# One fixed step list for all engines of a fused attention and gMLP kernel, with its own buffer rings, contiguous-write transposes, masks by affine select on GpSimd, and v by a casting DMA

## The chip, the cores and the metric

The kernel runs on one core of one Trainium2 chip. The time is device time of that core, in microseconds (us). Most executions of one kernel lie within a few per cent (the kernel before 244.14 to 247.13 us). An execution more than 1.5% above the fastest of its kernel is called slow here, and the ratios use fast runs alone.

The engines are named as in the profile: PE (the tensor engine's matmuls), PEld (its weight loads), DVE (VectorE), ACT (ScalarE), POOL (GpSimd), SP (SyncE, which only issues DMAs here). Each engine has its own list of instructions here, and the engines wait for each other by semaphores: in the kernel before, GpSimd waited 62.7 us in all at one line (L301) for results of DVE. A wait also holds up what stands behind it in the list. So the order in which a program is written down for one engine can cost time on another.

## The reference, cut

Sliding-window attention with four sink keys feeds a gated MLP whose gate mixes along the sequence. Shapes: 4 batches, 8 heads, 768 positions, head size 64, so a model width of 512.

```python
# attention, per batch and head: q, k, v are (768, 64)
scores = q @ k.T / sqrt(64)
keep   = (key < 4) | ((0 <= query - key) & (query - key < 128))
a      = softmax(where(keep, scores, -1e9))
x      = heads_side_by_side(a @ v)              # (4, 768, 512)

# gMLP
h      = gelu_tanh(x @ w_in)                    # 512 -> 1024
u, v   = h[..., :512], h[..., 512:]
v_n    = (v - mean(v)) / sqrt(var(v) + 1e-6) * g_ln
v_s    = einsum('ts,bsd->btd', w_sg, v_n) + b_sg[None, :, None]   # w_sg is 768 x 768
out    = x + (u * v_s) @ w_out
```

## The kernel before

The kernel computes in bf16 with float32 sums. A helper for each stage is called in interleaved Python loops; the framework then reorders instructions by its own scheduler and gives out buffers from pools. Heads go in pairs `p`, 0 to 3. `T` makes the transposed q and k of a pair, `QK` the scores and their exponentials, `AV` the attention output, `MV` and `MU` the two halves of the first MLP layer, `WT` the transposed `w_sg`, `SP` the product with it, `OUT` the last layer.

```python
ps_sc = ctx.enter_context(tc.tile_pool(name="ps_sc", bufs=2, space=bass.MemoryType.PSUM))  # 2 banks each
ps_av = ctx.enter_context(tc.tile_pool(name="ps_av", bufs=2, space=bass.MemoryType.PSUM))
ps_mm = ctx.enter_context(tc.tile_pool(name="ps_mm", bufs=2, space=bass.MemoryType.PSUM))

def T(b, p):
    q32, k32, v32 = staged.pop((b, p))          # float32, loaded by SyncE's queue
    for name, src in (("q", q32), ("k", k32)):
        cb = cast.tile([128, NT, 2, Dh], BF16, name=name + "b")
        pcast(cb..., src...)                    # GpSimd: float32 -> bf16          [cut]
        ps = ps_mm.tile([128, NT, 128], BF16, name="trp", tag="mm")
        for t in range(NT):                     # NT = 6
            nc.tensor.transpose(ps[:, t, :], cb[:, t, :, :].rearrange("p h d -> p (h d)"), iden)
        dst = trs.tile([128, S], BF16, name=name + "T")
        dv = dst.rearrange("p (i t) -> p t i", t=NT)     # row 6*i + t sits at i*6 + t
        if name == "q":
            nc.vector.tensor_copy(dv, ps)
        else:
            nc.scalar.copy(dv, ps)
    pcast(v_sb[b % 2][:, 2 * p:2 * p + 2, :, 0:Dh], v32...)   # GpSimd casts v       [cut]
    # ... sink columns of k: 2 small DVE copies

def QK(b, p, g):
    # ... matmuls into sc, two PSUM banks
    nc.scalar.activation(out=pt[:, :, 0:w], in_=sc[:, :, 0:w], func=AF.Exp, scale=scale)
    m = (mask0 if g == 0 else mask1)[:, 0:w]
    nc.vector.tensor_mul(pt[:, :, 0:w], pt[:, :, 0:w], m.unsqueeze(1).to_broadcast([128, 2, w]))

def MV(b, jj):
    # ... matmuls into hp
    nc.scalar.activation(out=vt, in_=hp, func=AF.Gelu_apprx_tanh)
    # ... bn_stats and bn_aggr on DVE -> mv; (var + 1e-6) ** -0.5 on GpSimd -> rs
    for jl in range(2):
        nc.vector.tensor_scalar(out=z[b][:, 2 * jj + jl, :], in0=vt[:, jl, :],
                                scalar1=mv[:, jl, 0:1], scalar2=rs[:, jl:jl + 1],
                                op0=ALU.subtract, op1=ALU.mult)

# the order, for each batch b [cut]
for n, m in enumerate(mu):          # mu: 3 x MV(b), 4 x MU(b)
    m()
    if n >= 2 and tu:
        tu.pop(0)()                 # tu: T of the next batch
if b == 0:
    for ti in range(NT):
        WT(ti)
# ... then the list of QK, AV, XT of batch b+1, mixed evenly with the SP and OUT of batch b
```

A row of q is loaded so that each partition holds six neighbouring positions, and the transposes put position 6*i + t into column i of block t. The copy to SBUF must restore the natural order. It reads the PSUM tile in order and writes each 2-byte value 12 bytes after the one before it.

The softmax here doesn't subtract the row's maximum and nothing guards it: scores larger than these inputs give would overflow.

## Time and profile before

The median was 245.59 us of 3 runs (244.14 to 247.13).

| | before |
|---|---|
| median of 4 | 246.18 us |
| span of the profiled run | 245.3 us |
| mean granted TensorE clock | 0.900 of full |
| busy PE / DVE / ACT / POOL | 74 / 73 / 55 / 39% |
| first matmul | 6.65 us |
| first matmul of the first MLP layer | 42.7 us |

The page of the kernel before opens with the busy time of each engine. Then comes the chain that ended last: the shares of the span by engine, and below that by line, when one goes back from the last instruction and asks at each step what released it.

```profile
PE 182.6 (74%) x1460; PEld 99.1 (40%) x1460; DVE 178.5 (73%) x302; ACT 135.2 (55%) x123; POOL 96.5 (39%) x134
...
DVE 37%; PE 27%; ACT 13%; POOL 8%; issue 6%; DMA 5%; SPq 2%; POOLq 0%; DVEq 0%; ACTq 0%
DVE qT L168 10%; DVE pt L206 9%; ACT kT L170 7%; PE hv L254 6%; PE ops L307 6%; POOL gatedT L301 5%; DVE z L271 5%; DMA v_104<-in_v_dram 4%; DVE gtmp L298 4%; ACT pt L204 4%; PE sc L199 3%; DVE st L265 3%; PE vs L294 3%; DVE ot L310 3%; PE scs L184 2%
```

No engine is close to full, and the chain changes engines all the time. That is the picture of engines that wait for one another in turn, DVE in front.

The groups of that page: line, engine, operation, output and input, shapes, number; after the first bar, busy us and mean ns of one; after the second, the idle time of that engine just before and what ended it.

```profile
L168 DVE COPY qT<-trp 128x768 bf16<-128x768 bf16 x16 | 43.5, 2718 | 12.4 <-PE trp L164 12.2
L170 ACT COPY kT<-trp 128x768 bf16<-128x768 bf16 x16 | 43.6, 2725 | 13.8 <-PE trp L164 13.8
...
L244 ACT COPY xT<-xps 128x768 bf16<-128x768 bf16 x16 | 12.8, 803 | 26.6 <-PE xps L243 26.6
...
L206 DVE TENSOR_TENSOR pt<-pt,mask_128 128x1024 bf16<-128x1024 bf16 (+1 forms) x32 | 25.8, 817 | 0.9 <-ACT pt L204 0.4
```

The same kernel's groups by form hold a further copy of the same size, on DVE, with contiguous bf16 on both sides in the inner dimension:

```profile
L335 DVE COPY wsgT<-wps 128x768 bf16<-128x768 bf16 x6 | 3.3, 558 | 2.4 <-PE wps L333 2.3
```

The q and k copies (L168, L170) take 2.72 us each. Two other copies of exactly 128x768 bf16 from PSUM take 0.80 us on ACT (L244) and 0.56 us on DVE (L335). What sets the q and k copies apart is the step of their writes.

A table of stretches, cut at the first MLP matmul of each batch. Columns: the stretch, its length, busy us of PE, PEld, DVE, ACT, POOL (instructions), granted clock, DMA share, GB/s.

```profile
0.00:42.70 42.70, 22.22 (x203) 12.72 (x204) 28.08 (x43) 26.03 (x23) 22.69 (x44) 0.88 1.00 236
42.70:105.80 63.10, 50.59 (x420) 29.42 (x419) 49.53 (x84) 34.42 (x32) 27.75 (x33) 0.84 0.59 157
105.80:160.50 54.70, 44.03 (x358) 23.20 (x356) 42.80 (x73) 33.36 (x30) 21.47 (x26) 0.88 0.32 92
160.50:211.60 51.10, 40.40 (x359) 22.23 (x356) 41.61 (x73) 33.09 (x30) 14.64 (x18) 0.97 0.09 32
211.60:245.30 33.70, 25.36 (x128) 11.56 (x125) 16.52 (x33) 8.29 (x9) 9.90 (x14) 0.98 0.16 58
```

In the two steady stretches (105.8 to 211.6) PE and DVE are each busy 84.4 us of 105.8. Each waits a fifth of the time, though not at the same moments.

### The profile page before, as it was taken

Reading aid. Unit: us, or ns where it says so; the run is one execution under the profiler, and the core shown is the slowest. Engines: PE = TensorE matmul, PEld = TensorE weight load, DVE = VectorE, ACT = ScalarE, POOL = GpSimd, SP = SyncE. Lnnn points to the kernel's source line nnn. Section 1 sums busy time; section 2 is a strip of 40 time slices with the busy share of each in tenths; the row PEclk is TensorE's granted clock in tenths of the full one; section 3 lists DMA queues with packets and bytes.
Section 4 is the critical chain, followed back from the end, with each engine's and each line's share of the span. In section 5 each row is a group of like instructions: output and inputs, shape, how many; then the busy total and the mean of one; then the engine's idle time right before and its main releaser. Section 6 shows DMA issues by size and latency. Waiting matters only on the chain.

```text
span 245.3 us, 3835 instructions
## 1 busy us (share of the span) xinstructions
PE 182.6 (74%) x1460; PEld 99.1 (40%) x1460; DVE 178.5 (73%) x302; ACT 135.2 (55%) x123; POOL 96.5 (39%) x134
## 2 busy tenths in 40 slices
PE   0457557892959979798478869898559698978892
PEld 0234333551634445445232336544234365534340
DVE  2775976788785789739993989739996888466553
ACT  2493768495953545166957736166979263455000
POOL 8619406526620645405750612413303315012550
PEclk9999875798575999999855999999889999999999
DMA  7969999999900028198700012120000030300033
GB/s 198 264 123 322 209 225 311 304 296 312 268 5 0 0 85 236 46 274 199 194 0 3 0 47 85 43 88 0 0 0 3 0 128 3 128 1 3 1 128 128
DMA packets 39778, 28.59 MB, mean 117 GB/s; under 512 B 26576, under 2 KB 36048, under 8 KB 39760
## 3 DMA queue, kind: packets, MB, share of 16 engines
q1 hardware_dynamic: 37920, 25.60, 37.2%
q0 software_dynamic: 1840, 2.75, 6.2%
q8 instruction: 11, 0.18, 0.3%
q14 instruction: 7, 0.06, 0.1%
HBM read 24.81 MB, written 6.29 MB: 127 GB/s over the span
## 4 chain that ended last, share of the span: by engine, by line
DVE 37%; PE 27%; ACT 13%; POOL 8%; issue 6%; DMA 5%; SPq 2%; POOLq 0%; DVEq 0%; ACTq 0%
DVE qT L168 10%; DVE pt L206 9%; ACT kT L170 7%; PE hv L254 6%; PE ops L307 6%; POOL gatedT L301 5%; DVE z L271 5%; DMA v_104<-in_v_dram 4%; DVE gtmp L298 4%; ACT pt L204 4%; PE sc L199 3%; DVE st L265 3%; PE vs L294 3%; DVE ot L310 3%; PE scs L184 2%
## 5 line engine op out<-in xcount | busy, mean ns | idle before, releaser
L204 ACT ACTIVATE pt<-sc 128x1024 bf16<-128x1024 f32 (+1 forms) x48 | 43.7, 954 | 27.6 <-PE sc L199 27.4
L301 POOL TENSOR_TENSOR gatedT<-gtmp,uT 128x384 bf16<-128x384 bf16 x32 | 33.2, 1042 | 64.8 <-DVE gtmp L298 62.7
L168 DVE COPY qT<-trp 128x768 bf16<-128x768 bf16 x16 | 43.5, 2718 | 12.4 <-PE trp L164 12.2
L170 ACT COPY kT<-trp 128x768 bf16<-128x768 bf16 x16 | 43.6, 2725 | 13.8 <-PE trp L164 13.8
L294 PE MATMUL vs<-wsgT,z 128*128 128x384 bf16 x192 | 38.6, 339 | 2.3 <-DVE z L271 1.1
L307 PE MATMUL ops<-w_out_sb,gatedT 128*128 128x512 bf16 x96 | 26.9, 381 | 11.8 <-POOL gatedT L301 10.3
L281 PE MATMUL hu<-xT,w_in_sb 128*128 128x384 bf16 x128 | 28.4, 373 | 0.5 <-ACT uT L284 0.2
L298 DVE SCALAR_TENSOR_TENSOR gtmp<-vs,g_sb,b_bc 128x384 bf16<-128x384 f32 x32 | 19.5, 610 | 12.0 <-PE vs L294 12.0
L244 ACT COPY xT<-xps 128x768 bf16<-128x768 bf16 x16 | 12.8, 803 | 26.6 <-PE xps L243 26.6
L254 PE MATMUL hv<-w_in_sb,xT 128*128 128x512 bf16 x96 | 24.6, 392 | 3.0 <-ACT vt L260 2.1
L206 DVE TENSOR_TENSOR pt<-pt,mask_128 128x1024 bf16<-128x1024 bf16 (+1 forms) x32 | 25.8, 817 | 0.9 <-ACT pt L204 0.4
L199 PE MATMUL sc<-qT,kT 64*128 64x256 bf16 x192 | 22.0, 305 | 4.4 <-ACT kT L170 4.2
L294 PEld LDWEIGHTS <-z 128*128 128x128 bf16 x192 | 17.7, 100 | 18.0 <-issue 6.9
L310 DVE TENSOR_TENSOR ot<-ops,x_sb 128x512 f32<-128x512 f32 x24 | 16.4, 689 | 11.2 <-PE ops L307 11.2
L164 PE MATMUL trp<-iden,qb 128*128 128x128 bf16 x96 | 10.2, 255 | 15.5 <-DVE qT L168 7.6
L219 PEld LDWEIGHTS <-pt 128*128 128x128 bf16 x192 | 16.0, 103 | 10.9 <-DVE pt L206 6.9
L271 DVE TENSOR_SCALAR z<-vt,mv,rs 128x512 bf16<-128x512 f32 x24 | 15.5, 689 | 4.3 <-POOL rs L269 4.3
L265 DVE BATCH_NORM_STATS2 st<-vt 128x6 f32<-128x512 f32 x24 | 15.5, 664 | 4.2 <-ACT vt L260 4.2
L235 DVE TENSOR_TENSOR x_sb<-av,rcp 128x384 bf16<-128x384 f32 x32 | 17.5, 555 | 0.8
L307 PEld LDWEIGHTS <-gatedT 128*128 128x128 bf16 x96 | 8.3, 97 | 24.1 <-POOL gatedT L301 15.8
L281 PEld LDWEIGHTS <-w_in_sb 128*128 128x128 bf16 x128 | 13.7, 110 | 10.3 <-issue 4.1
L284 ACT ACTIVATE uT<-hu 128x768 bf16<-128x768 f32 x16 | 15.1, 941 | 4.2 <-PE hu L281 4.2
(115 smaller groups left out, 276.6 us busy)
## 6 DMA issues: line engine op xcount, KB each, us to landing
out_dram<-ot SPq DMA_DIRECT2D x24, 256.0 KB
wsg_rows<-in_moe_w_sg_dram POOLq DMA_DIRECT2D x1, 1152.0 KB, 12.8
w_in_sb<-in_moe_w_in_dram POOLq DMA_DIRECT2D x1, 1024.0 KB, 11.2
w_out_sb<-in_moe_w_out_dram POOLq DMA_DIRECT2D x1, 512.0 KB, 9.8
q_94<-in_q_dram SPq DMA_DIRECT2D x1, 384.0 KB
k_96<-in_k_dram SPq DMA_DIRECT2D x1, 384.0 KB
v_98<-in_v_dram SPq DMA_DIRECT2D x1, 384.0 KB
q_100<-in_q_dram SPq DMA_DIRECT2D x1, 384.0 KB
```

What stands on the lines that cost most here:

```text
L168: nc.vector.tensor_copy(dv, ps)
L170: nc.scalar.copy(dv, ps)
L199: nc.tensor.matmul(sc[:, hl, 256 * jl:256 * jl + n], kT[b, p][rows, 128 * j:128 * (j + 1)], qT[b, p][rows, 128 * j:128 * j + n], start=Tru ...
L204: nc.scalar.activation(out=pt[:, :, 0:w], in_=sc[:, :, 0:w], func=AF.Exp, scale=scale)
L206: nc.vector.tensor_mul(pt[:, :, 0:w], pt[:, :, 0:w], m.unsqueeze(1).to_broadcast([128, 2, w]))
L254: nc.tensor.matmul(hp[:, jl, :], xT[b][:, c, 128 * j:128 * (j + 1)], w_in_sb[:, c, d_half:2 * d_half], start=(c == 0), stop=(c == KD - 1))
L271: nc.vector.tensor_scalar(out=z[b][:, 2 * jj + jl, :], in0=vt[:, jl, :], scalar1=mv[:, jl, 0:1], scalar2=rs[:, jl:jl + 1], op0=ALU.subtrac ...
L281: nc.tensor.matmul(hp[:, hf, 0:NH], w_in_sb[:, c, 128 * dc:128 * (dc + 1)], xT[b][:, c, NH * hf:NH * (hf + 1)], start=(c == 0), stop=(c == ...
L294: nc.tensor.matmul(ps[:, 0:NH], z[b][:, si, 128 * dc:128 * (dc + 1)], wsgT[:, si, NH * hf:NH * (hf + 1)], start=(si == 0), stop=(si == NT ...
L298: nc.vector.scalar_tensor_tensor(out=tmp, in0=ps[:, 0:NH], scalar=g_sb[:, dc:dc + 1], in1=b_bc[:, NH * hf:NH * (hf + 1)], op0=ALU.mult, op ...
L301: nc.gpsimd.tensor_mul(gatedT[b, hf][:, dc, :], tmp, uT[b][:, dc, NH * hf:NH * (hf + 1)])
L307: nc.tensor.matmul(ps, gatedT[b, hf][:, dc, 128 * tl:128 * (tl + 1)], w_out_sb[:, dc, :], start=(dc == 0), stop=(dc == KU - 1))
```

## The change

The intent is to take work off DVE and ACT, to spread it so that PE becomes the fullest engine, and to fix the order of every engine by hand so that the waits go. It has these parts:

1. **Contiguous writes.** The q and k copies write in order and read the PSUM tile with a step instead.
2. **Masks.** For batches 1 to 3 and groups 1 and 2 (24 of the 48 masks) two affine selects on GpSimd replace the DVE multiply.
3. **z.** Four of the six tiles of a batch are normalised on ACT (scale and bias) rather than on DVE; two more tiny GpSimd operations make the bias.
4. **v.** A DMA issued by GpSimd casts v to bf16 on the way; the float32 staging and the GpSimd casts go.
5. **Sinks.** Fewer and wider operations; `w_in` is loaded in two halves.
6. **Order and rings.** A list of some 700 steps replaces the loops and the scheduler. Each step is a small part of one old helper, and buffers come from rings: two PSUM tiles of two banks for scores and MLP, four of one bank for all else (before 2 and 2).

```diff
-            dv = dst.rearrange("p (i t) -> p t i", t=NT)
-            if name == "q":
-                nc.vector.tensor_copy(dv, ps)
-            else:
-                nc.scalar.copy(dv, ps)
+    def EQ(b, p):
+        dst = qT.new((b, p))
+        nc.vector.tensor_copy(dst.rearrange("p (i t) -> p i t", t=NT),
+                              psb(("q", b, p)).rearrange("p t i -> p i t"))
+    def EK(b, p):                       # the same with nc.scalar.copy            [cut]
+
+    def MK(b, p, g):
+        if g == 0 or b == 0:
+            ...                         # the DVE multiply as before              [cut]
+            return
+        nc.gpsimd.affine_select(out=p4[:, :, :, 0:128], in_=p4[:, :, :, 0:128], ...)
+        nc.gpsimd.affine_select(out=p4[:, :, 0:nj, 128:256], in_=p4[:, :, 0:nj, 128:256], ...)
+
+    ZACT = 4
+    def Z(b, j):
+        if j < ZACT:
+            nc.scalar.activation(out=zt[:, j, :], in_=vt[b, jj][:, jl, :], func=AF.Identity,
+                                 bias=nmr[:, jl:jl + 1], scale=rs[:, jl:jl + 1])
+        else:
+            nc.vector.tensor_scalar(...)                                        # [cut]
+
+    def LV(b, i):
+        nc.gpsimd.dma_start(out=v_sb[b % 2][:, hs, :, 0:Dh]..., in_=v[b, hs]...)  # [cut]
+
+    sc_ring = Ring("sc", 2, [128, 2, 512], F32, psum)
+    mm_ring = Ring("mm", 4, [128, 512], F32, psum)
+
+STEPS = """
+IDEN LC ZERO LQ.0.0 LK.0.0 LV.0.0 LQ.0.1 LK.0.1 VSK MASK VSM CQ.0.0 CK.0.0 TQ.0.0 EQ.0.0 LQ.0.2 LV.0.1 LK.0.2 TK.0.0
+... [some 700 steps; name.batch.index; L loads, C casts, T transposes, E copies out of PSUM, WT/WE those of w_sg]
+"""
+    with tc.manual_schedule():
+        for step in STEPS.split():
+            name, *idx = step.split(".")
+            code[name](*(int(i) for i in idx))
```

`LC` at the head of the list issues ten small loads (eight of sink rows of v, then `g_ln` and `b_sg`) on SP, ahead of the first load of q.

## The prediction

> **What bounds it now.** No engine is full: busy shares on the page are PE 74%, DVE 73%, ACT 55%, POOL 39%. The chain of waits is DVE 37%, PE 27%, ACT 13%, POOL 8%; its largest lines are the qT copy (10%), the mask multiply (9%) and the kT copy (7%). So this is in-order engines waiting for each other, DVE the fullest. Stretches between the first MLP matmuls of each batch: head 42.7 us, then 63.1, 54.7, 51.1, tail 33.7. In the 51.1 stretch DVE is busy 41.6, PE 40.4, ACT 33.1, POOL 14.6.
>
> **What the change does**, costed from the groups by form:
>
> 1. *qT/kT copies.* 128x768 bf16 from PSUM, written with a 12-byte step: 2.72 us on DVE and on ACT, 16 each. Contiguous bf16 evictions of that size take 0.80 us (xT, ACT) and 0.56 us (wsgT, DVE). Now the write is contiguous and the PSUM read strided. [...] estimate 0.9 us on DVE, 0.82 on ACT. Saves 29 us DVE, 30 us ACT. No run yet shows a strided PSUM read.
> 2. *Masks.* 24 of 48 leave DVE (0.99 and 0.64 us: 19 us saved). POOL gets 48 affine selects; from 0.19 us at 8 columns and 0.285 at 128, 0.58 us at 512 (estimate): +25 us POOL.
> 3. *z.* 16 of 24 go from DVE (0.69 us) to ACT (0.75, estimate): -11 DVE, +12 ACT; POOL gets 24 more tiny ops (+6).
> 4. *v.* 16 POOL casts of 0.83 us vanish (-13); 10 casting DMAs issued by POOL at about 1 us each replace them.
> 5. *Sinks.* 32 small DVE copies become 16 multiplies; the POOL multiply (5 us) goes to DVE.
> 6. *Order and rings.* Every engine's order is rewritten; four one-bank PSUM buffers in place of 2+2; w_in is loaded after most of batch 0; the next batch's transposes and scores spread over the gating stage.
>
> Sums (estimates): DVE 178 to about 118, ACT 135 to 117, POOL 96 to 114. PE has the same 2922 instructions. When dense, matmuls issue every 162 ns (384 columns), 216 ns (512), 30 ns (AV), so PE needs about 35 us a batch; other engines then need 29 to 31.
>
> **Critical path.** Per batch the fullest engine falls from 42 (DVE) to 35 (PE); before, the stretch was 1.23 times the fullest. With the same ratio: 42 to 43 per steady batch, 46 for the first (wsg transposes, loads). Head: q starts about 4 us later, behind ten small issues on SP (0.45 us each), but w_in no longer competes and copies are short: 36. Tail: 28. Sum 36+46+42+43+28 = 195.
>
> **Prediction: 195 us, 183 to 212. Faster by over 2%: 0.96; within: 0.025; slower: 0.015.**
>
> **Right or wrong.** Groups: EQ near 0.9 us, EK near 0.82; affine selects near 0.58; z on ACT near 0.75. Page: PE the fullest (above 80%), DVE about 60%, ACT 60%, POOL above 55%. Granted clock mean above the present 0.90. The chain should be led by PE, the q/k copies below 5% of it. The first transpose should come near 10 to 11 us (6.65 now), yet the first MLP matmul earlier than 42.7.
>
> **What would make it wrong.** A strided PSUM read as slow as the strided write (then 215 to 225). POOL late with masks or casts, [...], or casting DMAs of 256-byte rows slower than I think, stretching the head. Or the fixed order assuming times the chip doesn't keep.

The 0.9 us is the guess, and the 29 us saved on DVE (16 x 1.82) rest on it. The record does not say what the 0.75 us for z was worked out from; in the trace of before an activation of 128x512 on ACT (`exs`) averaged 0.595 us. That trace also holds what the other estimates start from: matmuls begin 162 to 163 ns apart with 384 columns (L281, L294), 215 to 216 with 512 (L254, L307) and 30 in `AV`; the three DMA issues on GpSimd took 0.80 to 0.98 us, and the first three on SP 0.43 to 0.46; the load of `w_in` was issued at 4.59 us and took 11.2 us to land, while the 16 DMA engines were busy 90% (0 to 12 us). That `w_in` and the first loads of q, k and v hindered each other there was the estimate; no run moved it alone.

## More of the kernel before

The DMA queues of the page (packets, MB, share of the span of 16 engines):

```profile
q1 hardware_dynamic: 37920, 25.60, 37.2%
q0 software_dynamic: 1840, 2.75, 6.2%
```

## The result, and the profile after

| | before | after |
|---|---|---|
| median of 4 | 246.18 us | 191.69 us (190.63 to 192.99) |
| span of the profiled run | 245.3 us | 190.1 us |
| granted clock, mean | 0.900 | 0.961 |
| busy PE / DVE / ACT / POOL, us | 182.6 / 178.5 / 135.2 / 96.5 | 155.3 / 124.8 / 115.2 / 120.7 |
| first matmul | 6.65 us | 12.22 us |
| first matmul of the first MLP layer | 42.7 us | 37.6 us |

The ratio is 0.7815 with a 95% interval of 0.7751 to 0.7879. A ratio here is the mean time of one kernel's fast runs over the mean of the other's fast runs of the same rounds, so it is not quite the ratio of the medians.

From the page after, the same lines as before, with two rows of the picture in 40 slices (tenths; PEclk is the granted clock):

```profile
PE 155.3 (82%) x1460; PEld 93.4 (49%) x1460; DVE 124.8 (66%) x254; ACT 115.2 (61%) x139; POOL 120.7 (64%) x192
...
PE   0037687630899999998999899999999999999990
...
PEclk9999789995599999999999999999999999999998
...
PE 58%; DMA 17%; POOL 15%; DVE 3%; SPq 2%; issue 1%; ACT 1%; POOLq 0%
PE mm L444 14%; DMA wsg_gated<-in_moe_w_sg_dram 13%; PE mm L461 11%; PE sc L380 10%; PE sc L424 8%; DMA k<-in_k_dram 4%; POOL q L178 4%; POOL k L178 3%; PE sc L299 3%; PE mm L255 3%; POOL wsg_gated L454 3%; PE mm L367 2%; PE mm L436 2%; PE mm L339 2%; POOL P L318 1%; POOL v_sb L174 1%
```

PE is now busy 82% of the span and leads the chain with 58%; the q and k copies are not among the chain's listed lines. One slice of PE's row is 0 in the first third, and the clock shows 5s beside it (a granted clock of 0.50 from 48.19 to 50.70 us). The chain names the load of `w_sg` with 13%.

PE's own busy time fell by 27.3 us (182.6 to 155.3) with the same 1460 matmuls. The higher mean clock, spread evenly over the busy time, would account for about 12 us of that (an estimate: 182.6 x 0.100 less 155.3 x 0.039); the rest is not explained here. No run sets the clock by itself, so whether it is a cause of the gain or follows from PE idling less was not tested. It can hardly be most of the 54 us: within one kernel, a_zdve below, the executions with mean clocks of 0.943 and 0.982 took 192.66 and 190.69 us, only 2 us apart.

The groups by form that answer to those of before:

```profile
L318 POOL TENSOR_SCALAR_AFFINE_SELECT P<-P 128x512 bf16<-128x512 bf16 x24 | 15.2, 635 | 4.0 <-ACT P L307 3.8
L265 DVE COPY qT<-mm 128x768 bf16<-128x768 bf16 x16 | 15.1, 948 | 8.9 <-PE mm L255 8.4 <-ACT xT L370 0.4
...
L174 POOL DMA_DIRECT2D v_sb<-in_v_dram x10 | 13.2, 1321 | 1.4 <-PE mm L285 0.8 <-DVE v_sb L238 0.7
...
L270 ACT COPY kT<-mm 128x768 bf16<-128x768 bf16 x16 | 12.9, 803 | 14.2 <-PE mm L255 14.2
...
L413 ACT ACTIVATE z<-vt,nmr,rs 128x512 bf16<-128x512 f32 x16 | 12.7, 811 | 0.9 <-POOL nmr L403 0.9
...
L322 POOL TENSOR_SCALAR_AFFINE_SELECT P<-P 128x256 bf16<-128x256 bf16 x12 | 5.5, 455 | 0.0
```

The q and k copies fell from 2.72 us to 0.95 and 0.80 us. The k copy on ACT costs what the contiguous copy of before cost (0.80), so reading PSUM with a step costs ACT nothing that shows. On DVE the copy with the stepped read took 0.95 us, and the contiguous one of before (L335) 0.56. Why DVE differs from ACT here was not tested.

The stretches after, cut in the same way, and last the whole from 66 us to the start of the last batch's MLP:

```profile
0.00:37.60 37.60, 18.37 (x228) 11.77 (x229) 24.96 (x52) 19.13 (x24) 26.35 (x41) 0.95 1.12 252
37.60:95.40 57.80, 48.03 (x485) 29.98 (x483) 37.09 (x73) 37.21 (x45) 37.37 (x54) 0.91 0.96 155
95.40:131.30 35.90, 35.09 (x345) 21.16 (x344) 24.77 (x53) 27.87 (x35) 28.79 (x49) 1.00 0.61 97
131.30:158.30 27.00, 27.00 (x266) 16.66 (x264) 19.91 (x44) 20.79 (x25) 17.01 (x30) 1.00 0.04 14
158.30:190.10 31.80, 26.76 (x144) 13.87 (x142) 18.06 (x33) 10.17 (x12) 11.20 (x20) 0.98 0.27 100
66.00:158.30 92.30, 90.22 (x936) 55.24 (x935) 68.76 (x145) 71.23 (x86) 73.56 (x114) 1.00 0.45 90
```

From 66 to 158.3 us PE is busy 90.2 us of 92.3, which is 98%. DVE, ACT and POOL are busy 69 to 74 us each. These are not waits in turn any more: PE is the limit of this part. The stretches are not comparable one to one with those of before, since the list pulls the next batches' transposes and scores forward, into the first long stretch.

PE's timeline where the row shows its 0 (start, busy us, and in brackets the idle time before and its releaser):

```profile
38.69 1.25 PE L380 MATMUL sc<-w_in_sb,xT 128*128 128x512 bf16 x5 [0.24 <-ACT xT L370]
48.19 2.74 PE L436 MATMUL mm<-iden,wsg_gated 128*128 128x128 bf16 x24 [8.25 <-DMA wsg_gated<-in_moe_w_sg_dram]
```

PE stands still for 8.25 us, until the load of `w_sg` has landed. GpSimd issued that load at 23.4 us and it took 24.7 us to land; in the kernel before it took 12.8. The queues show why it may: the software queue, which carries it, now has 27,104 packets and 5.90 MB. (In the kernel before it had 1,840 packets and 2.75 MB, the size of the three weight loads that GpSimd issued: 1152, 1024 and 512 KB.)

```profile
q0 software_dynamic: 27104, 5.90, 36.9%
q1 hardware_dynamic: 12992, 19.31, 30.5%
```

An estimate of a packet's cost, from these lines and those of before: the hardware queue lost 24,928 packets and 532 us of engine time (37.2% of 16 x 245.3 us, less 30.5% of 16 x 190.1 us), so a plain 256-byte row of v took about 21 ns. The software queue gained 25,264 packets and 879 us in the same reckoning, about 35 ns for a row that is cast on the way.

### The profile page after: what moved, and what is told of

Its sections match the earlier page's. It is cut to its first block, busy times and chain, and to the rows that moved or that the text cites. A ratio compares the mean times of both kernels' runs of the same rounds, so it can differ in the third digit from the quotient of the medians.

```text
span 190.1 us, 3794 instructions
## 1 busy us (share of the span) xinstructions
PE 155.3 (82%) x1460; PEld 93.4 (49%) x1460; DVE 124.8 (66%) x254; ACT 115.2 (61%) x139; POOL 120.7 (64%) x192
## 3 DMA queue, kind: packets, MB, share of 16 engines
q0 software_dynamic: 27104, 5.90, 36.9%
q1 hardware_dynamic: 12992, 19.31, 30.5%
## 4 chain that ended last, share of the span: by engine, by line
PE 58%; DMA 17%; POOL 15%; DVE 3%; SPq 2%; issue 1%; ACT 1%; POOLq 0%
PE mm L444 14%; DMA wsg_gated<-in_moe_w_sg_dram 13%; PE mm L461 11%; PE sc L380 10%; PE sc L424 8%; DMA k<-in_k_dram 4%; POOL q L178 4%; POOL k L178 3%; PE sc L299 3%; PE mm L255 3%; POOL wsg_gated L454 3%; PE mm L367 2%; PE mm L436 2%; PE mm L339 2%; POOL P L318 1%; POOL v_sb L174 1%
## 5 line engine op out<-in xcount | busy, mean ns | idle before, releaser
L307 ACT ACTIVATE P<-sc 128x1024 bf16<-128x1024 f32 (+1 forms) x48 | 44.1, 964 | 12.9 <-PE sc L299 11.9
L454 POOL TENSOR_TENSOR wsg_gated<-gtmp,uT 128x384 bf16<-128x384 bf16 x32 | 31.3, 987 | 11.6 <-DVE gtmp L449 10.9
L444 PE MATMUL mm<-wsgT,z 128*128 128x384 bf16 x192 | 33.9, 326 | 0.0
L449 DVE SCALAR_TENSOR_TENSOR gtmp<-mm,g_sb,b_bc 128x384 bf16<-128x384 f32 x32 | 19.4, 614 | 12.3 <-PE mm L444 11.7
L380 PE MATMUL sc<-w_in_sb,xT 128*128 128x512 bf16 x96 | 23.3, 388 | 0.2 <-ACT xT L370 0.2
L461 PE MATMUL mm<-w_out_sb,wsg_gated 128*128 128x512 bf16 x96 | 23.2, 379 | 0.0
L424 PE MATMUL sc<-xT,w_in_sb 128*128 128x384 bf16 x128 | 22.3, 326 | 0.0
L314 DVE TENSOR_TENSOR P<-P,mask 128x1024 bf16<-128x1024 bf16 (+1 forms) x24 | 18.8, 795 | 1.3 <-ACT P L307 1.2
L339 PE MATMUL mm<-v_sb,P 128*128 128x65 bf16 x192 | 17.1, 196 | 2.5 <-DVE P L314 2.4
L359 DVE TENSOR_TENSOR x_sb<-mm,rcp 128x384 bf16<-128x384 f32 x32 | 17.8, 557 | 1.1
L299 PE MATMUL sc<-qT,kT 64*128 64x256 bf16 x192 | 16.4, 275 | 2.5 <-ACT P L307 1.3
## 6 DMA issues: line engine op xcount, KB each, us to landing
wsg_gated<-in_moe_w_sg_dram POOLq DMA_DIRECT2D x1, 1152.0 KB, 24.7
w_in_sb<-in_moe_w_in_dram POOLq DMA_DIRECT2D x2, 512.0 KB, 19.2
```

Source lines behind the costliest of these rows:

```text
L299: nc.tensor.matmul(sc[:, hl, 256 * jl:256 * jl + n], kT[b, p][rows, 128 * j:128 * (j + 1)], qT[b, p][rows, 128 * j:128 * j + n], start=Tru ...
L307: nc.scalar.activation(out=pt[:, :, 0:w], in_=sc_ring[b, p, g][:, :, 0:w], func=AF.Exp, scale=scale)
L339: nc.tensor.matmul(av[:, il, hl, :], P[b, p, i // 2][:, hl, 256 * (i % 2):256 * (i % 2) + 128], vb[:, h, i, :], start=first, stop=False)
L359: nc.vector.tensor_mul(xs[:, 3 * half:3 * half + 3, 128 * p:128 * (p + 1)].rearrange("p t (h d) -> p t h d", h=2), av[:, :, :, 0:Dh], rcp. ...
L380: nc.tensor.matmul(hp[:, jl, :], xT[b][:, c, 128 * j:128 * (j + 1)], w_in_sb[:, c, d_half:2 * d_half], start=(c == 0), stop=(c == KD - 1))
L424: nc.tensor.matmul(hp[:, hf, 0:NH], w_in_sb[:, c, 128 * dc:128 * (dc + 1)], xT[b][:, c, NH * hf:NH * (hf + 1)], start=(c == 0), stop=(c == ...
```

## The experiments

Twelve kernels ran. All outputs are right. Names that begin with `b_` start from the kernel before, those with `a_` from the kernel after. Three theories stood against each other for the 54 us: (1) work taken off DVE and ACT, above all the 12-byte steps; (2) the order and rings, which turn idle time to use; (3) both together, neither enough without the other. Ratios are always to the kernel before, run on the same chip in the same rounds. The medians are over all runs of a kernel, slow ones included. The readings rest on the fast runs and on whether all runs of one kernel lie above all runs of another.

| run | median us | ratio to before | 95% interval |
|---|---|---|---|
| after | 191.69 | 0.7815 | 0.7751–0.7879 |
| b_contig | 223.02 | 0.9137 | 0.9040–0.9234 |
| b_ops | 237.23 | 0.9597 | 0.9465–0.9729 |
| b_v | 222.45 | 0.9088 | 0.9043–0.9133 |
| b_mz | 236.32 | none (3 of 4 slow) | |
| a_oldops | 218.52 | 0.8915 | 0.8838–0.8992 |
| a_strided | 211.89 | 0.8697 | 0.8607–0.8787 |
| a_dvemask | 195.84 | 0.7951 | 0.7805–0.8096 |
| a_zdve | 190.91 | 0.7792 | 0.7753–0.7830 |
| a_vhw | 194.01 | 0.7910 | 0.7843–0.7976 |
| a_wtlate | 181.74 | 0.7402 | 0.7337–0.7466 |
| a_qfirst | 190.48 | 0.7767 | 0.7700–0.7834 |
| best | 183.26 | 0.7439 | 0.7401–0.7478 |

### b_contig: the contiguous copies alone, in the old kernel

```diff
-            dv = dst.rearrange("p (i t) -> p t i", t=NT)
+            dv = dst.rearrange("p (i t) -> p i t", t=NT)
+            ps = ps.rearrange("p t i -> p i t")
```

> Kernel before, with only the q and k copies turned to contiguous writes (strided PSUM reads). The copies should take 0.95 us on VectorE and 0.80 us on ScalarE as in the changed kernel, not 2.72. Theory 1 (the copies sat on the chain of waits, 17% of it, and most of that comes back): 213 to 222 us. Theory 2 (the order of the old kernel is what limits; removing DVE and ACT work only uncovers the next wait): 228 to 240 us.

Measured: 223.02 us (221.91 to 226.83). The page's chain by engine, and its q and k copies:

```profile
DVE 33%; PE 19%; DMA 18%; POOL 11%; issue 6%; SPq 6%; ACT 4%; POOLq 1%; DVEq 0%; ACTq 0%
...
L169 DVE COPY qT<-trp 128x768 bf16<-128x768 bf16 x16 | 15.2, 951 | 17.9 <-PE trp L164 17.7
...
L171 ACT COPY kT<-trp 128x768 bf16<-128x768 bf16 x16 | 12.9, 805 | 11.2 <-PE trp L164 11.2
```

The copies take 951 and 805 ns, as in the new kernel, so their cost belongs to the write order and not to the new rings. The gain of 23 us leaves the time 1 us above the range of the first theory (213 to 222) and 5 us below that of the second. DVE lost 26 us of work (178.5 to 152.5) and ACT 29; which of the two copies gave more of the 23 us was not tried apart. DVE still leads the chain.

### b_ops: all changed operations, in the old order and pools

```diff
 (b_contig, and in it:)
+        if g == 0 or b == 0:           # masks: DVE only here, else 2 affine selects on GpSimd
+        nc.gpsimd.tensor_tensor(nmr, rs, mv[:, :, 0], op=ALU.mult)           # z: 4 of 6 tiles on ACT
+                nc.scalar.activation(out=z[b][:, 2 * jj + jl, :], in_=vt[:, jl, :], func=AF.Identity,
+                                     bias=nmr[:, jl:jl + 1], scale=rs[:, jl:jl + 1])
-        nc.sync.dma_start(out=v32, ...)  and its pcast
+        nc.gpsimd.dma_start(out=v_sb[b % 2]..., in_=v[b, 2 * p:2 * p + 2]...)
```

> Kernel before with all changes of operations (contiguous copies, masks by affine select on GpSimd for groups 1 and 2 of batches 1 to 3, four of six z tiles on ScalarE, v by casting DMA), but its old emission order, its scheduler and its pools. If the operations carry the gain: 190 to 200 us. If the order and the rings carry a good part: 205 to 220 us, with engine busy sums like those of the changed kernel (DVE about 122, ACT about 116, GpSimd about 120) and TensorE idle between them.

Measured: 237.23 us (233.77 to 243.17; two of four runs slow, the two fast ones 233.8 and 233.9). That is slower than was expected: with **more** work taken off DVE it loses to b_contig, whose slowest run took 226.83. The busy line of its page (this profile fell on a slow run, 238.7 us span), and three groups with what they waited for; last, the first two of these groups in b_contig:

```profile
PE 172.6 (72%) x1460; PEld 93.8 (39%) x1460; DVE 124.2 (52%) x262; ACT 117.2 (49%) x139; POOL 127.7 (53%) x206
...
L324 PE MATMUL ops<-w_out_sb,gatedT 128*128 128x512 bf16 x96 | 29.0, 407 | 15.2 <-POOL gatedT L318 13.9
...
L298 PE MATMUL hu<-xT,w_in_sb 128*128 128x384 bf16 x128 | 28.8, 386 | 9.4 <-ACT vt L270 9.4
...
L285 ACT ACTIVATE z<-vt,nmr,rs 128x512 bf16<-128x512 f32 x16 | 12.1, 805 | 22.0 <-POOL nmr L282 21.6
```

```profile
L308 PE MATMUL ops<-w_out_sb,gatedT 128*128 128x512 bf16 x96 | 28.0, 393 | 10.6 <-POOL gatedT L302 9.3
...
L282 PE MATMUL hu<-xT,w_in_sb 128*128 128x384 bf16 x128 | 24.5, 336 | 0.7 <-ACT uT L285 0.7
```

DVE, ACT and POOL have nearly the same busy time as in the kernel after (124, 117, 128 against 125, 115, 121), and the fast runs of b_ops are some 42 us longer. What grew is waiting in a ring of engines. ACT waits 21.6 us for the bias that GpSimd makes (`nmr`), PE waits 9.4 us for ACT (`vt`) and 13.9 us for GpSimd (`gatedT`). In b_contig PE waited 0.7 and 9.3 us at these two places; the 13 us more are about what the fast runs of b_ops lose to it (11 us). In the kernel after, the same group of z on ACT waits 0.9 us for `nmr` (L413 above). From 104.6 to 204.3 us PE was busy 82.2 us of 99.7, while DVE, ACT and POOL were busy only 55, 58 and 52.

### b_v and b_mz: which of the operations hurts in the old order

b_v is b_contig with the casting DMA for v alone; b_mz is b_contig with the masks and z moved, and v as it was. The edits are the corresponding lines of b_ops.

> Old kernel with contiguous copies (223 us) and v by casting DMA, issued in the old order, where the transposes of each pair are emitted; no other change. If the late issue of v is what made all operations together worse than the contiguous copies alone (237 against 223): 230 to 238 us. If it is masks and z instead: 219 to 226 us.

> Old kernel with contiguous copies (223 us), masks of groups 1 and 2 on GpSimd and four of six z tiles on ScalarE; v as before. If these, put behind GpSimd's other work and into ScalarE's queue by the old order, cost more than they save: 228 to 238 us. If v was the cause: 212 to 222 us.

Measured: b_v 222.45 us (219.19 to 224.01), the same as b_contig (223.02). So the casting DMA by itself is not the cause. b_mz took 236.32 us (230.83 to 237.51). Three of its four runs count as slow, so no ratio of fast runs is given; but its one fast run, the fastest, took 230.83, and that is above every run of b_contig and of b_v. The masks and z together are the cause. Two groups of b_mz, and ACT's timeline in a place where it happens:

```profile
L299 PE MATMUL hu<-xT,w_in_sb 128*128 128x384 bf16 x128 | 29.0, 389 | 10.2 <-ACT vt L271 10.2
...
L286 ACT ACTIVATE z<-vt,nmr,rs 128x512 bf16<-128x512 f32 x16 | 12.1, 806 | 18.1 <-POOL nmr L283 17.8
```

```profile
108.90 3.13 ACT L286 ACTIVATE z<-vt,nmr,rs 128x512 bf16<-128x512 f32 x4 [3.16 <-POOL nmr L283]
111.93 1.00 ACT L271 ACTIVATE vt<-hv 128x1024 f32<-128x1024 f32 x1
```

ACT waits 3.16 us at the head of its queue for `nmr`, carries out four z, and only then the next gelu (`vt`) at 111.93 us. PE had finished the tile of that gelu at about 106.4 us, by its own timeline. PE in turn waits 10.2 us in all at L299 for such a gelu, because its two-bank PSUM tiles are not free. In this place GpSimd did the eight tiny operations behind `nmr` from 107.33 to 110.47 us and no affine select stood ahead of them: the old order puts z directly behind its statistics, so that ACT now waits for DVE and GpSimd with a gelu behind it in its queue. Which of the two moves, masks or z, weighs more in the sum was not tried apart and stays open.

### a_oldops: the new list and rings with the old operations

```diff
-        nc.vector.tensor_copy(dst.rearrange("p (i t) -> p i t", t=NT), psb(...).rearrange("p t i -> p i t"))
+        nc.vector.tensor_copy(dst.rearrange("p (i t) -> p t i", t=NT), psb(...))      # and k
-        if g == 0 or b == 0:
+        if True:                                                                      # all masks on DVE
-    ZACT = 4
+    ZACT = 0                                                                          # all z on DVE
-        nc.gpsimd.dma_start(out=v_sb..., in_=v...)
+        nc.sync.dma_start(out=v32.new((b, p)), in_=v...)   # and a new step CV, the GpSimd cast
```

> The new step list and rings with the old operations: strided q and k writes, all masks and all z tiles on VectorE, v by plain DMA and GpSimd cast. Busy sums go back to about those of before (DVE 175, ACT 132). If the order alone is worth something without the operations: 218 to 232 us, with DVE nearly full in the steady stage. If order and operations only work together: 238 us or more.

Measured: 218.52 us (216.49 to 218.92), all fast. The fewer sink operations and the split `w_in` load stayed as in the kernel after. So the list and rings are worth 28 us with the old operations. A stretch in its middle (columns as above):

```profile
60.00:175.00 115.00, 94.48 (x873) 56.15 (x871) 100.19 (x169) 83.85 (x75) 55.31 (x73) 0.94 0.34 95
```

DVE is busy 100.2 us of 115, 87%: here DVE is the fullest engine, and with the durations of this trace no order can bring this stretch below those 100.2 us.

With b_ops these runs make a square of four:

| | old order and pools | new list and rings |
|---|---|---|
| old operations | 1 | 0.8915 |
| new operations | 0.9597 | 0.7815 |

If the two parts acted each on its own, the product would be 0.8556, or 0.856 x 246 = 211 us. The measured 191.7 us is 19 us less. So the operations as a whole and the list do more together than apart, as theory (3) says, but "neither enough without the other" does not hold. With b_contig in place of b_ops the product is 0.9137 x 0.8915 = 0.8146, or 200.5 us: the copies alone (23 us) and the list alone (28 us) add up to 51 of the 54 us. What needs the list is the moves of masks and z, which lose time in the old order. The list with the contiguous copies and nothing else was not run, so what the other moves bring there is not measured directly. The square is not quite clean: b_ops leaves out the change of the sinks, and a_oldops keeps it.

### a_strided, a_dvemask, a_zdve: one operation at a time put back in the new list

```diff
 (a_strided)
-        nc.vector.tensor_copy(dst.rearrange("p (i t) -> p i t", t=NT), psb(...).rearrange("p t i -> p i t"))
+        nc.vector.tensor_copy(dst.rearrange("p (i t) -> p t i", t=NT), psb(...))      # and k
 (a_dvemask)
-        if g == 0 or b == 0:
+        if True:
 (a_zdve)
-    ZACT = 4
+    ZACT = 0
```

> Changed kernel with only the strided writes of q and k put back. DVE busy rises by 28 us and ACT by 31 us, so both are fuller per batch (about 37 and 38 us) than TensorE (35). Theory that fullest-engine work sets the time: 208 to 218 us. Rival, that the new order hides it: below 200 us.

> Changed kernel with all masks as multiplies on VectorE (no affine selects on GpSimd). GpSimd busy falls by 28 us, DVE rises by about 20 us. Since DVE at 145 us stays below TensorE's 155 and GpSimd led the chain between 66 and 90 us, I expect the same time within 2%: 188 to 195 us. Rival, that moving the masks off DVE was needed: 197 us or more.

> Changed kernel with all z tiles on VectorE (16 more of 0.55 to 0.69 us, DVE busy 135) and none on ScalarE (16 fewer of 0.81 us, ACT busy 103). Both stay below TensorE, so 189 to 194 us, the same within 2%. If z on ScalarE was needed: 196 us or more.

Measured: a_strided 211.89 us (210.62 to 213.34), a_dvemask 195.84 us (192.37 to 196.96, two of four slow), a_zdve 190.91 us (190.69 to 192.66). The chain of a_strided by engine, and by line:

```profile
PE 47%; ACT 24%; POOL 9%; issue 6%; DVE 5%; DMA 4%; SPq 2%; ACTq 0%; POOLq 0%; DVEq 0%
ACT kT L269 14%; PE mm L442 10%; PE mm L459 8%; PE sc L378 7%; PE sc L422 5%; PE sc L297 5%; ACT P L305 4%; DMA k<-in_k_dram 4%; PE mm L255 3%; DVE qT L265 3%; PE mm L337 2%; ACT z L411 2%; POOL P L316 2%; ACT uT L427 2%; PE mm L365 2%
```

The 12-byte steps alone cost 20 us in the new list: with them ACT's k copy takes 14% of the chain. The masks on DVE cost perhaps 3 us by the ratios of the fast runs (0.7951 and 0.7815) and perhaps nothing, since the intervals overlap. The z on DVE cost nothing that shows (0.7792). Masks and z were not put back together. DVE's busy time rose to 132.8 us with z back and to 140.2 with the masks back, still below PE's 155. In this list an engine that was not the limit could be given some work back at little or no cost. One more comparison: a_strided differs from a_oldops (218.52 us) by masks, z and v alone, with strided copies in both, and there these moves together brought 6.6 us.

### a_vhw: v by SyncE's queue and a GpSimd cast, in the new list

The edit is the v part of a_oldops alone: `LV` becomes plain loads on SP into a ring of four float32 tiles, with a cast step `CV` behind each `CK`.

> Changed kernel with only v loaded as float32 by SyncE's queue and cast on GpSimd (0.83 us each). In the two traces a 256-byte v row costs about 36 ns of a DMA engine when cast and about 22 ns when not (estimate from the queues' shares). If that slows the first 48 us, the w_sg load lands earlier than 48 us and TensorE's 8 us wait for it shrinks: 185 to 190 us. Rival: GpSimd, which leads the chain between 66 and 90 us, gets 13 us more work and the time is equal or longer: 191 to 197 us.

Measured: 194.01 us (193.08 to 195.15). Two groups of its trace:

```profile
L181 POOL TENSOR_SCALAR v_sb<-v 128x768 bf16<-128x768 f32 x16 | 14.1, 879 | 19.2 <-DMA v<-in_v_dram 19.2
...
L444 PE MATMUL mm<-iden,wsg_gated 128*128 128x128 bf16 x36 | 2.6, 233 | 2.3 <-DMA wsg_gated<-in_moe_w_sg_dram 2.3
```

`w_sg` landed 14.3 us after its issue instead of 24.7, and PE waited 2.3 us for it instead of 8.2. In a_oldops, where v is also on SyncE's queue, it took 16.1 us, and in a_wtlate and a_qfirst, with the casting DMA, 24.8 and 25.0. So the cast rows of v in the software queue do hold up `w_sg`; whether by the cast or by the shared queue was not tried apart. Yet GpSimd now waited 19.2 us for the plain v loads, and the ratio was 1% worse, with intervals that overlap (though all four runs lie above those of the kernel after). So the casting DMA is at most a small gain, with a cost beside it.

### a_wtlate: the transposes of w_sg later

Only the list changes. All `WT` and `WE` steps go from among the first `MV` steps to behind the first-layer matmuls of batch 0:

```diff
-... MV.0.0 CQ.1.0 WT.0 GV.0.0 LQ.2.0 WT.1 CK.1.0 WE.0 WT.4 WT.3 WE.1 MV.0.2 CQ.1.1 WE.4 WE.3 ... WT.5 CQ.1.2 WT.2 ...
+... MV.0.0 CQ.1.0 GV.0.0 LQ.2.0 CK.1.0 MV.0.2 CQ.1.1 ... Z.0.3 MU.0.1
+WT.0 WT.1 WE.0 WE.1 WT.4 WT.3 WE.4 WE.3 WT.5 WT.2 WE.5 WE.2 CK.1.2 GU.0.2 ...
```

> Changed kernel with the w_sg transposes moved behind all first-layer matmuls of batch 0 in the step list, nothing else. TensorE idles 8.2 us at the w_sg load while about 9 us of first-layer matmuls of batch 0 are ready behind it. If that wait is on the critical path: 183 to 187 us. If the wait only moves, because the gating needs w_sg soon after: 189 to 192 us.

Measured: 181.74 us (181.30 to 184.29), 0.7402 of before, 10 us below the kernel after. Its page's busy line and clock row, and the group of these transposes; below them the same group in the kernel after:

```profile
PE 153.6 (85%) x1460; PEld 92.0 (51%) x1460; DVE 124.7 (69%) x254; ACT 115.4 (64%) x139; POOL 120.7 (67%) x192
...
PEclk9999999999999999999999999999999999999999
```

```profile
L436 PE MATMUL mm<-iden,wsg_gated 128*128 128x128 bf16 x36 | 2.2, 219 | 0.0
```

```profile
L436 PE MATMUL mm<-iden,wsg_gated 128*128 128x128 bf16 x36 | 3.6, 282 | 8.2 <-DMA wsg_gated<-in_moe_w_sg_dram 8.2
```

No wait is left there. In the kernel after, PE stood at a transpose whose data had not come, while the matmuls of `MV` and `MU` behind it were ready. The gain is larger than the 8.2 us of wait. The transposes took 282 ns each after the wait and 219 ns without it, PE's busy time fell by 1.7 us, and the mean clock of the profiled runs rose from 0.961 to 1.00 (fast runs: 0.961 to 0.978 before the move, 0.987 to 1.00 after it). In the kernel after the granted clock averaged 0.62 from 40.00 to 48.19 us, while PE stood still, 0.50 from 48.19 to 50.70 us, during the first 24 of these transposes, and 1.00 from 66 to 95.4 us; the clock row of a_wtlate shows no 5s. That the standing still lowered the clock was not tested by itself.

### a_qfirst: the small loads behind the first q and k

```diff
-IDEN LC ZERO LQ.0.0 LK.0.0 LV.0.0 ...
+IDEN ZERO LQ.0.0 LK.0.0 LC LV.0.0 ...
```

> Changed kernel with the ten small constant loads issued after the first q and k loads instead of before them. The first q load is issued at 0.8 us instead of 4.6, the first transpose comes near 8.5 us instead of 12.2. If the whole chain of the head starts earlier and the w_sg load is issued earlier with it: 187 to 189 us. If the w_sg load's landing at 48 us does not move, the gain is lost in that wait: 190 to 192 us.

Measured: 190.48 us (189.54 to 191.75), 0.7767. The first transpose came at 7.62 us instead of 12.22, the first MLP matmul at 35.28 instead of 37.63, and `w_sg` landed at 45.93 instead of 48.19; PE still waited 8.34 us for it. Of 4.6 us gained at the start 2.3 were left at the first MLP matmul and about 1 at the end, within the interval of the kernel after. The start was not the limit: PE still stood until `w_sg` had landed.

### best: both list edits, and the sink products later

a_wtlate, with the ten small loads behind the first two pairs of q and k (the sink rows) and behind the last pair (`g_ln`, `b_sg`), and the sink products `VSM` moved behind the first mask, so that no q copy waits behind them.

> Changed kernel with the w_sg transposes behind all first-layer matmuls of batch 0 (worth 10 us alone), the small constant loads behind the first two pairs' q and k loads, and the sink products on VectorE behind the first masks, so that VectorE's first q copy does not wait for a constant. The first transpose should come near 7.6 us instead of 12.2 and the first MLP matmul 3 to 4 us earlier. If the two gains add: 177 to 180 us. If the head's gain is lost in later waits: 181 to 182 us.

Measured: 183.26 us (180.91 to 185.02; five rounds), 0.7439 against 0.7402 for a_wtlate: no better. PE's timeline in the head:

```profile
20.44 0.35 PE L341 MATMUL mm<-v_sb,P 128*128 128x65 bf16 x3 [6.76 <-DVE P L316]
```

The first transpose came at about 7.6 us, but PE then stood 6.76 us for a mask on DVE. The eight sink operations of all four batches, 14.49 to 19.75 us on DVE, stood in its queue ahead of the second mask. The first MLP matmul came at 38.4 us, no sooner than in the kernel after. The gain had become a new wait, by a fault of placement in this experiment. a_wtlate stays the fastest kernel measured. Whether splitting the sink products by batch would bring the last 4 us was not tried.

## Why the prediction was right, point by point, and where it was not

**The time.** 195 us predicted, 191.69 measured, inside the range of 183 to 212.

**Durations.** They were near: the q copy 0.9 predicted, 0.95 measured; the k copy 0.82 and 0.80; an affine select of 512 columns 0.58 and 0.635 (0.455 for 256); z on ACT 0.75 and 0.81. The issue of a casting DMA was put at 1 us and took 1.32.

**Sums.** DVE 118 predicted, 124.8 measured; ACT 117 and 115.2; POOL 114 and 120.7. PE is the fullest at 82%, the chain is led by PE with 58%, and the clock is 0.961, as written.

**The head.** 36 predicted, 37.6 measured; the first transpose 10 to 11, and 12.22 measured. The ten issues ahead of q did cost what was said (the first load of q was issued at 4.59 us instead of 0.80), and a_qfirst shows that they hardly matter for the end.

**What failed: "With the same ratio: 42 to 43 per steady batch".** The prediction carried the ratio of stretch to fullest engine (1.23) from the old order over to the new. In the new list it is 92.3 over 90.2, or 1.02, from 66 to 158.3 us. That is what a fixed order is for, and the prediction gave it no worth. The other side of the same fault: b_ops shows that the new operations in the old order would not have brought the 42 to 43 us, since fewer busy microseconds on DVE and ACT came back as waits for GpSimd. So the gain was never a matter of the fullest engine alone. The split 36 + 46 + 42 + 43 + 28 was measured as 37.6 + 57.8 + 35.9 + 27.0 + 31.8. The second term is 12 us too low, and the next two together 22 us too high. A part of this only moves work between stretches, since the list draws the next batches forward. So the total came out right partly by luck: errors of both signs cancelled.

**What was not foreseen: the wait for `w_sg`.** The prediction named slow casting DMAs as a risk, "stretching the head". They did not stretch the head. They held up another load in the same queue (24.7 us to land, and 14.3 us with v on the other queue in a_vhw), and PE waited 8.25 us for it in the second stretch; a_wtlate shows that the list's early transposes turned that into 10 us.

**Risks that did not come.** A strided read of PSUM as slow as the strided write: no, 0.95 and 0.80 us against 2.72. The durations of DVE's masks did not grow with more work on GpSimd: those of 1024 columns left on DVE averaged 0.80 us, against 0.86 and 0.99 us for the two masks before. But when the two work at the same time, both traces show longer operations. In the kernel before, the 21 such masks that overlap an operation of GpSimd averaged 1.05 us and the 11 others 0.70 us. In the kernel after, GpSimd's 8 casts of 128x768 that overlap a mask on DVE averaged 1.05 us and the 24 others 0.83 us, none of these above 0.85. (A longer one also overlaps more easily.) What this costs in the whole was not tested by itself.

**Shown and not shown.** Shown: the contiguous writes pay in both orders (23 us in the old, 20 us in the new); the moves of masks and z hurt in the old order, and in the new one putting either back cost no more than about 3 us by the fast runs; the list and rings are worth 28 us with the old operations and some 42 us with the new (fast runs of b_ops, 233.8 and 233.9, against 191.7). Not run: the list with the contiguous copies alone, and masks and z apart in the old order. Only argued: how much of the list's worth is order and how much is the rings, since no run had one without the other. The clock was not set apart from either.

## What to carry to other kernels

When no engine is full and the chain of waits goes round all of them, count for each moved operation not only its busy time but what stands behind it in its new queue; the moves of masks and z that the new order bears cost about 8 us or more in the old one. A copy that writes 2-byte values with a step like the 12 bytes here is the first thing to mend, since it paid in every order tried (2.72 us a copy against 0.95 on DVE and 0.80 on ACT; 23 us of the whole in the old order, 20 us in the new). After such a change look for the one place where the newly fullest engine stands still with ready work behind it: moving twelve steps of the list there brought a further 10 us.
